# Second attention layer: first matrix blocks loaded in half-steps 48 to 50; first chunk's last block transposed within the output product

## The chip, the cores and the metric

The kernel runs on one core of one Trainium2 chip. The metric is the device time of one execution in microseconds (us): the median of several runs. The engines are named as in the profile: PE (matrix products), with PEld for its weight loads, DVE (VectorE), ACT (ScalarE), POOL (GpSimd) and SP (SyncE, which here only issues DMAs). A line number such as L955 is that of the kernel before.

## The reference, cut to what matters

Four layers, each with a residual sum: local dilated attention (A), Fourier mixing (B), and both once more. Everything is float32; S = 2048 rows, D = 640 columns.

```python
def _A_ref(x, wqkv, wo):
    H = 32; Dh = 20; W, dil = 8, 2
    qkv = (x @ wqkv).reshape(B, S, 3, H, Dh).transpose(2, 0, 3, 1, 4)
    ...
    logits = jnp.einsum("bhsd,bhswd->bhsw", q, kg) * scale
    logits = jnp.where(mask, logits, -1e9)
    attn = _softmax(logits, axis=-1)
    o = jnp.einsum("bhsw,bhswd->bhsd", attn, vg)
    return o.transpose(0, 2, 1, 3).reshape(B, S, D) @ wo

def _B_ref(x, dft_seq_re, dft_seq_im, dft_hid_re, dft_hid_im):
    a = jnp.einsum("bsd,ed->bse", x, dft_hid_re)
    b = jnp.einsum("bsd,ed->bse", x, dft_hid_im)
    return jnp.einsum("ts,bse->bte", dft_seq_re, a) - jnp.einsum("ts,bse->bte", dft_seq_im, b)

x = A_x
x = x + _A_ref(_layernorm(x), A_wqkv, A_wo)
x = x + _B_ref(_layernorm(x), ...)
x = x + _A_ref(_layernorm(x), A_wqkv, A_wo)
x = x + _B_ref(_layernorm(x), ...)
```

kg and vg hold, for each row, the keys and values of the eight rows 0, 2, ... 14 places before it.

## The kernel before

**Tiles and precision.** The rows lie in 4 chunks (c) of 4 blocks (j) of 128 rows. Float32 products are made of three passes over a high and a low half: a tile is split into a rounded high part (a cast on ACT) and the rest (a subtraction on DVE or POOL), and PE sums high by high, high by low and low by high.

**An attention layer** (`layer_a`; layers 0 and 2) runs in half-steps from -7 to 66. Half-step 2u + jp handles head group and chunk u, pair jp. Work is put into a plan, a dictionary by half-step and phase, with `at(step, phase, ...)`; the phases of a half-step are then played in a fixed order (PHASES), so each engine's queue has an order written out by hand. In a half-step stand: QKV products (`qkv_mm`, L362) with their evacuation by ACT (`qkv_evac`, L369) and stores; window loads of keys and values (`w_load`, L417, tile `win`, 5 buffers); the DVE products of `qk_mul` (L431) and `av_mul` (L469) with POOL's additions (L433, L484 to L486); the softmax; the output product with `wo` (`wo_mm`, L509) and the residual sum (`wo_add`, L159, stored by L523); layer norms of finished blocks (L884 and L888 make the high and low part of `xn`).

**The first z product.** The tail of an attention layer already does the first of the products of the Fourier layer behind it: z = xn transposed by one column block of the Fourier matrix, over 16 blocks of rows, z(0) to z(15), 15 matmuls each (`z_mm`, L955). `ZTHIRDS` says in which half-steps the thirds of each z(s) stand; for the second attention layer z(0) stands in half-step 50, z(1) and two thirds of z(2) in 51. A matrix block comes as a raw load (`c_load`, L911), a cast (`c_hi`, L915) and a subtraction (`c_lo`, L942) in the first attention layer, and ready-made as 512 KB from the DRAM buffer `c0b` (`c_get`, L933) in the second, one half-step before its first use. Its tile goes by `c_tag` into one of s0, s2 and s3 in turn, each a single buffer. The same buffers hold transposed blocks before: s2 and s3 blocks 2 and 3 of the last chunk's input, s0 the attention output of chunk 1's last block, which `wo_mm` reads in half-steps 48 and 49. A load into a buffer waits for the last reader of what was there, and SP issues its DMAs in order.

**Between the layers.** `early` (in `layer_a`) prepares chunk 0 of the second attention layer inside the last part of the Fourier layer (`LayerB.pair`): through hooks it loads, normalises and transposes blocks 0 to 3 (`xt`: PE transposes at L225 into the bank `pq`, a high part by ACT at L232, a low part by DVE at L236; each block in two parts, 2 and 3 transposes). The hooks ("y", k) stand behind the k-th fifth of the last y product, 12 matmuls each (`ymm`, L1033), and "end" behind everything. In `pair` only PE's order is given by hand; there, and where the two layers meet, a scheduler merges the two lists and orders the other engines. After a y product `yout` adds its banks to the residual (L1046, DVE) and takes its statistics (L151 and L153, ACT). `zt_put` (L1010 to L1015) splits a finished z into its two parts. In the last layer `x_whole` (L1078) adds the two parts of a stretch of `xn` again, into s1 or s2.

Of the kernel before, what the change touches and what calls it, by code (L numbers as in the profile page):

```python
# [28 lines left out]
NJ = 4  # L29
# [45 lines left out]
def tile_layers(ctx: ExitStack, tc: tile.TileContext, x, wqkv, wo, cs, wre, wim, out):  # L75
# [136 lines left out]
    def a_weights_q(q):  # L212
        wt = T([P, 2, KD, 3 * F], f"r1_{q}", F32R)
        for k in range(KD):
            split(wt[:, 0, k], wt[:, 1, k], wq_load1(q, k))
        return wt
# [25 lines left out]
    def layer_a(li, stats, handoff, prev):  # L242
# [21 lines left out]
        def at(step, phase, fn, *args):  # L264
            plan.setdefault((step, phase), []).append((fn, args))
# [5 lines left out]
        def x_load(c, j, tag="xa"):  # L271
            xnT[(c, j)] = load_x(xin[c], j, tag)
# [9 lines left out]
        def x_norm(c, j, fast=False):  # L282
            stats[c].apply(j, xnT[(c, j)], fast)

        def xt_pe(c, j, part, bank):
            if part == 0:
                xnT[(c, j, 1)] = T([P, 2, KD, P], f"s{j}", F32R)
            xnT[(c, j, "p", part)] = t_pe(xnT[(c, j)], part, bank)

        def xt_hi(c, j, part):  # L290
            t_hi(xnT[(c, j, 1)], part, xnT[(c, j, "p", part)])

        def xt_lo(c, j, part):
            t_lo(xnT[(c, j, 1)], part, xnT[(c, j, "p", part)])
# [278 lines left out]
        def early():  # L573
            def x_get(j):
                x_load(0, j)
                x_norm(0, j)

            def w0():
                with tc.issue_after(prev.dma.ins):
                    wq[0] = a_weights_q(0)  # L580

            def xt(j, part):
                xt_pe(0, j, part, "pq")
                xt_hi(0, j, part)
                xt_lo(0, j, part)

            prev.pair(
                NPAIR - 1,
                stats,
                {  # L590
                    2: lambda: (x_get(0), x_get(1)),
                    4: lambda: xt(0, 0),
                    5: lambda: (xt(0, 1), x_get(2)),
                    6: lambda: xt(1, 0),
                    7: lambda: (w0(), xt(1, 1), x_get(3)),
                    ("y", 1): lambda: xt(2, 0),
                    ("y", 2): lambda: xt(2, 1),
                    "end": lambda: (xt(3, 0), xt(3, 1)),
                },
            )  # L600
            for q in range(1, NQ):
                wq[q] = a_weights_q(q)
# [63 lines left out]
        if not first:  # L666
            early()
# [48 lines left out]
        for u in range(NG):  # L716
# [9 lines left out]
            for jp in range(2):  # L726
                s = 2 * u + jp
# [21 lines left out]
        for c in range(2):  # L749
# [10 lines left out]
            for j in range(NJ):  # L760
                t = LNS[ly][c] + (2 - c) * j
# [46 lines left out]
        for z in range(len(thirds) // 3):  # L808
            t = thirds[3 * z]
            if first and z in PRE:  # L810
                at(max(thirds[3 * z - 7] + 1, t - 3), "dmac", handoff.c_get, z)
            elif first:
                at(t - 2, "dmac", handoff.c_load, z)
                at(t - 1, "hi", handoff.c_hi, z)
                at(t - 1, "misc", handoff.c_lo, z, z < NJ)
            else:
                at(t - 1, "dmac", handoff.c_get, z)
            for p in range(3):
                at(thirds[3 * z + p], "pe3", handoff.z_mm, z, p)
        if first:  # L820
# [44 lines left out]
    class LayerB:  # L865
# [35 lines left out]
            nc.vector.tensor_scalar(self.xl[(c, j)], xr[(c, j)], nmean, rstd, op0=ALU.add, op1=ALU.mult)  # L901

        def c_tag(self, s, t=0):
            tags = ("s3", "s0", "s2") if self.li == 1 else ("s0", "s2", "s3")
            if t:
                return (tags[0], tags[-1 if self.li == 3 else 1])[s % 2]
            return tags[s % 3] if s < NST - 1 else "s1"

        def c_load(self, s, t=0):
# [382 lines left out]
    st0 = [None] * NC  # L1292
    b1, b2 = LayerB(1), LayerB(3)
    layer_a(0, st0, b1, None)
    st2 = [None] * NC
    b1.run(st2)
    layer_a(2, st2, b2, b1)
    b2.run(None)
    b2.ytile(NT - 1, 0, None)
# [56 lines left out]
```

## Time and profile before

| | us |
|---|---|
| three runs | 1796.40, 1798.74, 1799.93 |
| median | 1798.74 |
| the profiled execution, its own time | 1789.91 |
| its span, first to last instruction | 1788.0 |
| mean granted PE clock in it | 0.994 |

The profile is of one execution. In a row of a timeline stand the start, the duration, the engine, the line, the operation, out<-in by the program's names, shapes and a count; in brackets the idle time of the engine just before, and what ended it. Rows of the windows view give a stretch, its length, then busy time (and instructions) of PE, PEld, DVE, ACT and POOL, the granted PE clock, the share of time that the DMA engines were busy, and GB/s. By the windows view the first attention layer lies at about 0 to 395 us, the Fourier layer behind it at 395 to 925, the second attention layer at 880 to 1280, the last layer from there on.

### The profile page before, as it was taken

To read this page: it belongs to the slowest core of one execution; us is meant where nothing else is said; L and a number is where in the kernel's file an instruction comes from. 1 tells how busy PE (TensorE), PEld (TensorE's weight loads), DVE (VectorE), ACT (ScalarE), POOL (GpSimd) and SP (SyncE) were. 2 spreads that over 40 slices of the span, in tenths; PEclk is the share of its full clock that TensorE was granted. 3 is DMA by queue.
4 is the path that set the end of the run, shared out by engine and by line. 5 is a ranking of instruction groups with operands and counts; after the bars stand their busy time and mean duration, and the time that the engine had idled before them with its cause. 6 is when DMAs were issued, how large, how long until landed. Compare 5 with 4: busy or idle time off the path is not lost.

```text
span 1788.0 us, 26460 instructions
## 1 busy us (share of the span) xinstructions
PE 1741.6 (97%) x8798; PEld 1507.1 (84%) x8798; DVE 1381.9 (77%) x2139; ACT 813.1 (45%) x1690; POOL 634.8 (36%) x593
## 2 busy tenths in 40 slices
PE   9999998989999999999999999999999999999999
PEld 7889887778888888888888889878787888888888
DVE  6999998887767767767738999989777677677673
ACT  4664544454445445445623344444534443443441
POOL 4899999940000000000017998889300000000000
PEclk9999999999999999999999999999999999999999
DMA  7896678758778687777737866687687766876761
GB/s 248 286 313 211 203 210 269 252 183 282 268 255 264 239 274 252 240 267 249 225 125 224 265 213 218 208 293 248 228 295 259 261 223 224 267 230 228 253 208 52
DMA packets 271849, 425.15 MB, mean 238 GB/s; under 512 B 22592, under 2 KB 150592, under 8 KB 271456
## 3 DMA queue, kind: packets, MB, share of 16 engines
q1 hardware_dynamic: 268512, 421.49, 71.6%
q10 hardware_dynamic: 3200, 1.97, 0.4%
q8 instruction: 70, 1.15, 0.3%
q14 instruction: 67, 0.55, 0.1%
HBM read 338.23 MB, written 85.14 MB: 237 GB/s over the span
## 4 chain that ended last, share of the span: by engine, by line
PE 62%; DVE 14%; POOL 12%; DMA 7%; issue 3%; ACT 2%; SPq 0%; DVEq 0%; ACTq 0%; POOLq 0%
PE aux L1033 13%; PE m L362 12%; PE m L1122 9%; PE t L1122 9%; PE pq L1122 5%; PE xt L1122 5%; POOL pr L484 4%; DVE pr L431 3%; POOL pr L433 3%; DMA win<-cs_in 2%; DVE pr L469 2%; POOL pr L485 2%; PE m L955 2%; PE aux L509 2%; PE t L955 2%
## 5 line engine op out<-in xcount | busy, mean ns | idle before, releaser
L362 PE MATMUL m<-r,s 128*128 128x480 f32 x1920 | 436.5, 382 | 2.1 <-ACT s L232 1.6
L362 PEld LDWEIGHTS m<-r,s 128*128 128x128 f32 x1920 | 355.2, 188 | 55.8 <-ACT s L232 2.6
L1115 ACT CAST r<-win 128x512 fp32r<-128x512 f32 x248 | 151.1, 620 | 172.6 <-DVE win L1151 81.1
L174 POOL TENSOR_TENSOR stats<-stats,mhalf 128x1 f32<-128x1 f32 (+1 forms) x40 | 29.8, 746 | 558.4 <-ACT stats L170 549.1
L1033 PE MATMUL aux<-r2a,zo 128*128 128x320 f32 x768 | 226.4, 309 | 0.0
L484 POOL TENSOR_TENSOR pr<-pr 128x640 f32<-128x640 f32 x126 | 205.9, 1634 | 33.8 <-DVE pr L469 33.2
L1033 PE MATMUL aux<-pr,zo 128*128 128x320 f32 x704 | 208.2, 308 | 0.0
L431 DVE TENSOR_TENSOR pr<-pq,win 128x1280 f32<-128x1280 f32 x128 | 189.8, 1483 | 16.4 <-ACT pq L404 12.3
L1116 DVE TENSOR_TENSOR r<-win,r 128x512 fp32r<-128x512 f32 x248 | 167.4, 688 | 45.0 <-ACT r L1115 43.5
L469 DVE TENSOR_TENSOR pr<-pq,win 128x1280 f32<-128x1280 f32 x128 | 190.9, 1491 | 4.3
L433 POOL TENSOR_TENSOR pr<-pr 128x640 f32<-128x640 f32 x128 | 183.3, 1432 | 16.5 <-DVE pr L431 16.3
L1122 PE MATMUL m<-r,r 128*128 128x512 f32 x606 | 156.4, 392 | 0.8 <-DVE r L1116 0.8
L1033 PEld LDWEIGHTS aux<-r2a,zo 128*128 128x128 f32 x768 | 144.1, 188 | 2.0
L1122 PEld LDWEIGHTS m<-r,r 128*128 128x128 f32 x606 | 113.5, 188 | 26.6 <-DVE r L1116 1.5
L1033 PEld LDWEIGHTS aux<-pr,zo 128*128 128x128 f32 x704 | 132.2, 188 | 2.1
L955 PE MATMUL m<-s,r 128*128 128x512 f32 x384 | 120.1, 400 | 13.4 <-POOL s L942 4.9
L1122 PE MATMUL t<-r,r 128*128 128x512 f32 x483 | 130.7, 393 | 2.0 <-issue 1.2
L955 PE MATMUL t<-s,r 128*128 128x512 f32 x384 | 119.1, 398 | 2.3 <-DVE ot L1015 1.5
L439 DVE TENSOR_REDUCE lg<-pr 128x64 f32<-128x640 f32 x128 | 103.9, 812 | 18.2 <-POOL pr L433 17.8
L485 POOL TENSOR_TENSOR pr<-pr 128x320 f32<-128x320 f32 x126 | 113.0, 897 | 9.9
L1151 DVE TENSOR_TENSOR win<-win,win 128x512 f32<-128x512 f32 x110 | 75.7, 690 | 45.7 <-DMA win<-cs_in 43.9
L1122 PEld LDWEIGHTS t<-r,r 128*128 128x128 f32 x483 | 90.5, 188 | 23.4 <-issue 1.6
(285 smaller groups left out, 3227.8 us busy)
## 6 DMA issues: line engine op xcount, KB each, us to landing
win<-cs_in SPq DMA_DIRECT2D x354, 256.0 KB, 4.2
r<-xc SPq DMA_DIRECT2D x240, 256.0 KB, 4.4
win<-kvb SPq DMA_DIRECT2D x96, 440.0 KB, 4.3
xa<-cs_in SPq DMA_DIRECT2D x122, 256.0 KB, 4.2
win<-kvb SPq DMA_DIRECT2D x64, 360.0 KB, 5.3
xc<-stg SPq DMA_DIRECT2D x40, 512.0 KB, 3.4
kvb<-stg SPq DMA_DIRECT2D x60, 320.0 KB, 4.7
xr<-xs SPq DMA_DIRECT2D x41, 320.0 KB, 3.6
```

The source lines that it names most:

```text
L362: nc.tensor.matmul(mt[g][:, : 3 * F], st[:, a, k], wq[q][:, b, k], start=n == 0, stop=n == 14)
L431: nc.vector.tensor_tensor(pr, q, wview(u, jp, 0, [[1, FE]]), op=ALU.mult)
L433: nc.gpsimd.tensor_tensor(pv[:, :, 0:10], pv[:, :, 0:10], pv[:, :, 10:20], op=ALU.add)
L439: nc.vector.tensor_reduce(lgs[u][:, 2 * jp : 2 * jp + 2].rearrange("p j w h -> p (j w h)"), prq.pop((u, jp))[:, :, 0:10], axis=AX.X, op=AL ...
L469: nc.vector.tensor_tensor(pr.rearrange("p j w (h d) -> p j w h d", d=DH), lgs[u][:, 2 * jp : 2 * jp + 2].unsqueeze(4).to_broadcast([P, 2, ...
L484: g.tensor_tensor(pr[:, :, 0:4], pr[:, :, 0:4], pr[:, :, 4:8], op=ALU.add)
L485: g.tensor_tensor(pr[:, :, 0:2], pr[:, :, 0:2], pr[:, :, 2:4], op=ALU.add)
L955: self.last = nc.tensor.matmul(self.z[t][k], self.xn[c][:, a, j, k * P : (k + 1) * P], self.ct[s][:, b], start=s == 0 and i == 0, stop=s = ...
L1033: self.last = nc.tensor.matmul(self.ym[e][:, :320], zt[(k, a, ri)][:, j2 * P : (j2 + 1) * P], w[:, e * 320 : (e + 1) * 320], start=(k, a, ...
L1115: nc.scalar.copy(hi, raw)
L1116: nc.vector.tensor_tensor(lo, raw, hi.bitcast(F32), op=ALU.subtract)
L1122: nc.tensor.matmul(bank, w(a, kb), hl[b], start=start and (a, b) == (0, 0), stop=stop and (a, b) == (1, 0),)
```

## The change

Four edits. The last two groups of transposes of `early` go from the hook "end" to the hooks ("y", 3) and ("y", 4). In the first attention layer the subtraction for z(11) and z(12) goes to POOL instead of DVE (`early=True` of `c_lo`). In the second, `c_get` for z(0), z(1) and z(2) is put into half-steps 48, 49 and 50 (before: 49, 50 and 50). And the tags of the last Fourier layer's first product begin with s2 instead of s0, while those of its second product stay as they were (s0, s3).

```diff
@@ early() @@
                     ("y", 1): lambda: xt(2, 0),
                     ("y", 2): lambda: xt(2, 1),
-                    "end": lambda: (xt(3, 0), xt(3, 1)),
+                    ("y", 3): lambda: xt(3, 0),
+                    ("y", 4): lambda: xt(3, 1),
@@ layer_a: the plan of the z products @@
             elif first:
                 at(t - 2, "dmac", handoff.c_load, z)
                 at(t - 1, "hi", handoff.c_hi, z)
-                at(t - 1, "misc", handoff.c_lo, z, z < NJ)
+                at(t - 1, "misc", handoff.c_lo, z, z < NJ or z in (11, 12))
             else:
-                at(t - 1, "dmac", handoff.c_get, z)
+                at(min(t - 1, 48 + z) if z < 3 else t - 1, "dmac", handoff.c_get, z)
@@ LayerB @@
         def c_tag(self, s, t=0):
-            tags = ("s3", "s0", "s2") if self.li == 1 else ("s0", "s2", "s3")
             if t:
-                return (tags[0], tags[-1 if self.li == 3 else 1])[s % 2]
+                return (("s3", "s0") if self.li == 1 else ("s0", "s3"))[s % 2]
+            tags = ("s3", "s0", "s2") if self.li == 1 else ("s2", "s0", "s3")
             return tags[s % 3] if s < NST - 1 else "s1"
```

## The prediction

> **What bounds the kernel now.** The page first: it says which engine has no room.
>
> ```profile
> span 1788.0 us, 26460 instructions
> PE 1741.6 (97%) x8798; PEld 1507.1 (84%) x8798; DVE 1381.9 (77%) x2139; ACT 813.1 (45%) x1690; POOL 634.8 (36%) x593
> ```
>
> PE is idle for 1788.0 − 1741.6 = 46.4 us in all, so an edit can win only by removing some of that idle time, or by removing stretches in which PE is busy but slow. I went from the waits of line 955 (z_mm) to the timelines around the four places where the two built programs differ. The windows view, one row for each stretch (last three columns: granted PE clock, DMA share, GB/s), shows the dearest place, the start of the second layer's z product:
>
> ```profile
> 1172.00:1174.00 2.00, 1.43 (x12) 1.19 (x10) 1.93 (x3) 1.49 (x5) 1.84 (x4) 1.00 0.00 0
> 1176.50:1183.00 6.50, 6.43 (x15) 4.74 (x15) 5.53 (x8) 1.78 (x6) 6.26 (x7) 0.54 1.00 335
> ```
>
> The DMA engines carry nothing from 1172 to 1174 and are then full; PE does 15 matmuls in 6.5 us at clock 0.54. PE's and SP's timelines say why:
>
> ```profile
> 1170.71 2.36 PE L509 MATMUL aux<-r2a,s 128*128 128x320 f32 x15
> 1173.96 0.44 PE L335 MATMUL t<-r,nident 128*128 128x384 f32 x1 [0.57 <-ACT r L331]
> 1176.47 2.92 PE L955 MATMUL m<-s,r 128*128 128x512 f32 x6 [2.07 <-DMA s<-c0b]
> 1184.12 0.73 PE L955 MATMUL m<-s,r 128*128 128x512 f32 x2 [1.19 <-DMA s<-c0b]
> 1190.07 1.04 PE L327 MATMUL aux<-ident,zo 128*128 128x128 f32 x8
> ...
> 1166.47 0.92 SPq L417 DMA_DIRECT2D win<-kvb  x2
> 1173.10 0.32 SPq L933 DMA_DIRECT2D s<-c0b  x1
> 1176.34 0.93 SPq L523 DMA_DIRECT2D xs<-xa  x1
> 1177.32 1.97 SPq L933 DMA_DIRECT2D s<-c0b  x2
> ```
>
> Block 0 is issued at 1173.10, when line 509 has finished with its old tenant of s0 (1170.71 + 2.36); PE waits 2.07 for it. Blocks 1 and 2 are issued behind the store of 1176.34; PE waits 1.19 for block 1. The lost time here is 2.07 + 1.19 + about 3.0 of half speed (15 matmuls from 1176.47 to 1182.93, 6.46; 25 take 1190.07 − 1184.12 = 5.95, so 15 at full clock 3.5) = 6.2 us.
>
> **Part 1, the blocks.** The rotation of tags for the second layer becomes s2, s0, s3. Block 0 goes to s2, free since the matmuls of the block before last, so its issue moves from 1173.10 to just ahead of the two window loads of 1166.47; it lands before the DMA engines fall idle. Block 1 now wants s0 and takes the place at 1173.10; block 2 stays behind the store of 1176.34, which waits for a VectorE add that nothing moves. From issue to use block 0 took 1176.47 − 1173.10 = 3.4 on idle DMA engines; block 1, by the chain of waits, 6.75 on full ones:
>
> ```profile
> 1177.32 6.75 DMA s<-c0b
> ```
>
> So z(0) runs from 1174.4 to 1177.9 without a wait, z(1), landed at 1176.5, to 1181.4, and z(2) waits for block 2: the bytes in front of it are those that stood in front of block 1, so it lands at 1177.32 + 6.75 = 1184.1. z(2) began at 1184.12 + 3.5 = 1187.6 before; PE is now 3.5 us ahead, but with a new gap of 1184.1 − 1181.4 = 2.7 us. What such a gap does to the clock:
>
> ```profile
> 356.56 6.12 PE L509 MATMUL aux<-r2a,s 128*128 128x320 f32 x30 [2.10 <-DVE xa L159]
> 307.03 4.56 PE L509 MATMUL aux<-r2a,s 128*128 128x320 f32 x30
> 282.92 1.43 PE L955 MATMUL m<-s,r 128*128 128x512 f32 x5 [1.91 <-POOL s L942]
> ```
>
> After 2.10 idle the same 30 matmuls took 1.56 more; after 1.91 the next five ran at full rate. Both gaps over 2 us brought half clock, so I charge 1.3 (1.56 less what falls into the gap itself): PE is 2.2 ahead at 1190.07. The Trainium skill ("TensorE: Matmul & The Clock Gate", Part 1: The HAM clock gate) has the clock halve only after at least one idle window of about 3.4 us; by that the charge would be 0 and the sum 0.8 better. The half rate agrees with 0.54 above; the 2.10 us gap does not agree with the length.
>
> Does the lead last? VectorE and GpSimd set the pace from 1190 on:
>
> ```profile
> 1189.14 1.49 DVE L431 TENSOR_TENSOR pr<-pq,win 128x1280 f32<-128x1280 f32 x1 [3.53 <-DMA win<-kvb]
> 1192.14 0.38 DVE L460 TENSOR_REDUCE pq<-lg 128x16 f32<-128x128 f32 x1 [1.51 <-ACT lg L447]
> 1195.35 1.58 POOL L484 TENSOR_TENSOR pr<-pr 128x640 f32<-128x640 f32 x1 [3.23 <-DVE pr L469]
> ```
>
> The 3.53 wait shrinks by what one block (512 KB at the 335 GB/s above, 1.5) no longer puts in front of the window load; L460 waits for ACT, whose exp stands behind copies of PE's transposes of 1190.07. So this chain comes 1.5 + 1.51 = 3.0 earlier at most, and 2.2 if PE is. I take **−2.2**; bounds 0 (nothing passes the attention chain) and −6.2 (block 2 in time, the clock stays up).
>
> **Part 2, the transposes.** The last block's two groups of PE transposes (2 and 3, line 225) move from after the y product into it. In the built order one more thing moves with them: ten of the second QKV group's matmuls (line 362) now stand before the last twelve of line 1033, where seven stood behind them.
>
> ```profile
> 891.35 0.39 PE L1033 MATMUL aux<-r2a,zo 128*128 128x320 f32 x1
> 894.94 1.69 PE L362 MATMUL m<-r,s 128*128 128x480 f32 x7
> 899.20 0.70 PE L362 MATMUL m<-r,s 128*128 128x480 f32 x2 [1.04 <-ACT s L232]
> 900.80 3.10 PE L362 MATMUL m<-r,s 128*128 128x480 f32 x13 [0.57 <-ACT s L232]
> ...
> 893.52 0.46 ACT L232 CAST s<-pq 128x384 fp32r<-128x384 f32 x1
> 896.19 0.89 DVE L1046 TENSOR_TENSOR xr<-aux,xr 128x320 f32<-128x320 f32 x2
> 897.11 0.74 ACT L151 ACTIVATE junk<-xr 128x640 bf16<-128x640 f32 x1 [1.28 <-DVE xr L1046]
> 898.80 0.35 ACT L232 CAST s<-pq 128x256 fp32r<-128x256 f32 x1
> 899.16 0.55 ACT L369 COPY stg<-m 128x480 f32<-128x480 f32 x1
> ```
>
> Two waits, 1.04 + 0.57 = 1.61, should go. But those ten need the copy of 893.52, done at 893.98. Twelve of line 1033 end at 891.35 + 1.8 = 893.15 (24 fill 891.35 to 894.94), so PE waits 0.85 there. Then ten matmuls (2.4 by the row of 894.94), the transposes and twelve of line 1033 (1.8) end at 898.3. In ACT's queue the copy of the second transposes stands behind L151, L369 and L153, and L151 waits for the adds behind line 1033's end: some 0.6 later (the second of the two adds, 0.45, and the hand-overs), 898.9. From L151 to the copy it is 898.80 − 897.11 = 1.69, plus 0.5 for the L369 now between: the copy runs from 901.1 to 901.55 and the 13 matmuls start at 901.6 instead of 900.80: **+0.8**. Bounds: −1.6 (both waits go, none comes) and +2.4 (0.8 and one halving, 1.56).
>
> **Part 3, blocks 11 and 12 of the first layer.** Their subtraction (line 942) moves from VectorE to GpSimd.
>
> ```profile
> L942 POOL TENSOR_TENSOR s<-stg,s x4: 1266/1272/1288, 281.6 to 304.4; 128x512 fp32r<-128x512 f32 x4
> L942 DVE TENSOR_TENSOR s<-stg,s x4: 681/1362/1903, 349.6 to 370.1; 128x512 fp32r<-128x512 f32 x4
> ...
> 363.39 0.49 DVE L159 SCALAR_TENSOR_TENSOR xa<-aux,xa 128x320 f32<-128x320 f32 x1 [0.84 <-DMA xa<-x_in]
> 368.76 0.62 ACT L915 CAST s<-stg 128x512 fp32r<-128x512 f32 x1 [4.48 <-DMA stg<-cs_in]
> 370.22 1.94 POOL L484 TENSOR_TENSOR pr<-pr 128x640 f32<-128x640 f32 x1 [1.81 <-DVE pr L469]
> 374.48 0.73 PE L955 MATMUL m<-s,r 128*128 128x512 f32 x2 [0.54 <-DVE r L888]
> 382.11 0.73 PE L327 MATMUL pq<-ident,zo 128*128 128x128 f32 x4 [0.89 <-POOL zo L486]
> ```
>
> VectorE is freed of about 1.36 twice, GpSimd gets 1.27 twice. The first is lost, since VectorE then waits for the load of 363.39 anyway. The second lets VectorE's next products, and the GpSimd work that waited 1.81 for them, start some 1.2 earlier; GpSimd's own 1.27 fits under those waits. PE's 0.54 goes, and the wait at 382.11 ends 0.9 earlier, since ACT, held by the load at 368.76, gives back a part. I take **−0.9**; bounds 0 and −1.4.
>
> **Part 4, an unnamed move.** With s2 free one block earlier, the first whole-tile sum of the last layer (line 1078) stands in VectorE's queue before the last head's tree (484 to 486), not after it.
>
> ```profile
> 1266.33 0.54 DVE L486 TENSOR_TENSOR zo<-pr 128x160 f32<-128x160 f32 x1
> 1267.15 0.60 PE L327 MATMUL pq<-ident,zo 128*128 128x128 f32 x4
> 1278.25 1.23 DVE L1078 TENSOR_TENSOR s<-r 128x1024 f32<-128x1024 f32 x1
> ```
>
> The tree ends at 1266.87, PE takes it at 1267.15; with 1.23 in front it ends at 1268.10: **+0.95** on PE. Where the sum stood, nothing waited for it. Bounds 0 and +1.3.
>
> **Sum:** −2.2 + 0.8 − 0.9 + 0.95 = −1.35 us. The profiled execution lasted 1789.91 (span 1788.0 and 1.9 around it), 8.8 below the median of the three runs, 1798.74; I carry the difference over unscaled: **1797.4 us**. From 0.2% (3.6 us; runs of before spread over 3.5) the difference can be told from none.
>
> **Rivals.** (a) *The clock stays up* in the new gap of part 1, as after the 1.91 gap: the lead is 3.0 and the sum −2.15: 1796.6. (b) *Block 2 lands in time*: its place in the queue improves by a block, the whole 6.2 is recovered: −6.2 + 0.85 = −5.35: 1793.4. For it: DMA is empty until 1174. Against: the issue behind the store at 1176.34 does not move. (c) *The transposes do what the change says*: −1.6 in place of +0.8, sum −3.75: 1795.0. For it: ACT's copy of the first transposes now comes before L151. Against: the copy of the second stands behind it. (d) *Slower*: the two new gaps of part 2 (0.85 and about 1.4, within 8.5 us) halve PE's clock there. Price 1.56 for one spell, 3.0 for one like 1176.5 to 1183; from 1.35 on the kernel is slower: up to 1800.4. Against: the present gaps there, 1.04 and 0.57, do nothing.
>
> **How the numbers follow.** Forecast 0.36, (a) 0.16, (b) 0.18, (c) 0.16, (d) 0.14. Faster by over 0.2% (below 1795.1) is nearly all of (b), half of (c) and, with the scatter of runs, a fifth of the forecast and (a): 0.35. Slower by over 0.2% (above 1802.3) needs (d) with scatter, or a bound of part 2 and part 4 together: 0.10. Within: 0.55. The range runs from (b) less its scatter, 1792.4, to (d), 1800.6.
>
> **What would show it.** In the changed profile: line 933's first row near 1166.5, no wait at z(0), clock 1.00 from 1174 to 1181, then a DMA wait of 2 to 3 before z(2); a line 362 wait of 0.85 near 893 and a larger one before the 13; PE's wait for VectorE near 374 gone; line 1078 before 484 and a wait of PE for line 486 near 1265. No wait before z(2), or none before the 13, would make it wrong.

## The result, and the profile after

| | before | changed |
|---|---|---|
| first series, median (20 runs each) | 1796.30 | 1791.13 |
| second series, median (28 and 10 runs) | 1793.12 | 1790.10 |
| the profiled execution, its own time | 1789.91 | 1791.85 |
| its span | 1788.0 | 1790.0 |

The ratio of changed to before is 0.9977, with a 95% interval of 0.9967 to 0.9986, in the first series and 0.9982 (0.9972 to 0.9993) in the second: 4.1 us and 3.2 us faster. The prediction said 1797.4 us and 1.35 us faster, so the sign was right, the gain too small, and 1791.13 lies 1.3 below the low end of the range, 1792.4. The two profiled executions stand the other way round: the one of before took 1789.91, 6.4 below the median of the twenty timed runs of before. The traces are therefore read stage by stage, and most of the work below is about what one execution can show. Line numbers above 598 are one higher in the changed kernel (942 becomes 943, 955 becomes 956, 1033 becomes 1034).

The page of the changed kernel, its span and busy times:

```profile
span 1790.0 us, 26461 instructions
PE 1740.7 (97%) x8798; PEld 1506.0 (84%) x8798; DVE 1380.2 (77%) x2137; ACT 813.0 (45%) x1690; POOL 636.4 (36%) x595
```

PE's idle time is 49.3 us, where it was 46.4. Nothing on the page tells the two kernels apart; the four stages do.

**Part 1.** Timelines of PE and of SP at the start of the second layer's z product:

```profile
1174.08 2.36 PE L509 MATMUL aux<-r2a,s 128*128 128x320 f32 x15
1177.61 1.56 PE L956 MATMUL m<-s,r 128*128 128x512 f32 x6
1181.11 0.63 PE L956 MATMUL m<-s,r 128*128 128x512 f32 x2
1187.64 0.73 PE L956 MATMUL m<-s,r 128*128 128x512 f32 x2 [2.86 <-DMA s<-c0b]
1191.00 1.70 PE L327 MATMUL aux<-ident,zo 128*128 128x128 f32 x8
...
1169.58 0.38 SPq L934 DMA_DIRECT2D s<-c0b  x1
1176.47 0.32 SPq L934 DMA_DIRECT2D s<-c0b  x1
1179.73 0.87 SPq L523 DMA_DIRECT2D xs<-xa  x1
1180.65 1.24 SPq L934 DMA_DIRECT2D s<-c0b  x1
```

Block 0 is asked for 4.5 us before the group of line 509 that held it back, so z(0) (1177.61) and z(1) start without a wait. Block 1 has taken the place behind that group (1176.47), block 2 stands behind the store, and PE waits 2.86 for it. From line 509 to line 327 it is 1191.00 − 1174.08 = 16.92, against 19.36 before: 2.44 less. Most of the lead lasts: from the same group to the 18 matmuls of line 509 near 1265 us it takes 1265.46 − 1174.08 = 91.38, against 1264.41 − 1170.71 = 93.70 before, 2.32 less.

**Part 2.** Timeline of PE where ten matmuls of line 362 now stand ahead of line 1034's last ones, and of ACT, which makes their operands; the last two rows are ACT's in the kernel before:

```profile
895.16 4.00 PE L362 MATMUL m<-r,s 128*128 128x480 f32 x10 [2.08 <-ACT s L232]
900.98 1.26 PE L362 MATMUL m<-r,s 128*128 128x480 f32 x5
904.22 3.10 PE L362 MATMUL m<-r,s 128*128 128x480 f32 x13 [1.65 <-ACT s L232]
...
892.85 0.60 ACT L126 ACTIVATE r<-win 128x480 fp32r<-128x480 f32 x1 [0.76 <-DMA win<-wqkv_in]
894.14 0.60 ACT L126 ACTIVATE r<-win 128x480 fp32r<-128x480 f32 x1 [0.24 <-DMA win<-wqkv_in]
894.65 0.46 ACT L232 CAST s<-pq 128x384 fp32r<-128x384 f32 x1
903.70 0.46 ACT L232 CAST s<-pq 128x384 fp32r<-128x384 f32 x1
```

```profile
891.87 0.60 ACT L126 ACTIVATE r<-win 128x480 fp32r<-128x480 f32 x1 [0.64 <-DMA win<-wqkv_in]
893.01 0.60 ACT L126 ACTIVATE r<-win 128x480 fp32r<-128x480 f32 x1
```

The first copy of line 232 ran from 893.52 before. Now it comes at 894.65. Two roundings of weights (line 126) stand ahead of it in both kernels; in this execution they start at 892.85 and 894.14 instead of 891.87 and 893.01, both of them when a load of weights lands. The two waits of 1.04 and 0.57 have become 2.08 and 1.65, and the ten matmuls took 4.00 where the row of seven at full clock (1.69) gives 2.4.

**Parts 3 and 4.** Timeline of PE at lines 889 and 486 in the first layer, then at line 486 in the second, and VectorE's rows for the latter:

```profile
372.46 0.73 PE L956 MATMUL m<-s,r 128*128 128x512 f32 x2 [0.25 <-DVE r L889]
380.10 0.73 PE L327 MATMUL pq<-ident,zo 128*128 128x128 f32 x4 [0.89 <-POOL zo L486]
1269.27 0.55 PE L327 MATMUL pq<-ident,zo 128*128 128x128 f32 x3 [0.38 <-DVE zo L486]
...
1265.05 1.65 DVE L1079 TENSOR_TENSOR s<-r 128x1024 f32<-128x1024 f32 x1
1266.62 1.49 DVE L484 TENSOR_TENSOR pr<-pr 128x640 f32<-128x640 f32 x1
1268.89 0.33 DVE L486 TENSOR_TENSOR zo<-pr 128x160 f32<-128x160 f32 x1
```

PE's wait for line 889 has shrunk from 0.54 to 0.25 and the wait for line 486 at 380.10 is still 0.89, but it ends 2.0 earlier. Of these 2.0, 1.45 are half clock that before had behind line 509's wait at 356 us and this execution has not (6.12 against 4.67 for the same 30 matmuls). In the second layer line 1079 stands ahead of the tree, whose end PE awaits; from the first group of line 509 (18 matmuls) to the second it took 3.80 before and 4.82 now, 1.02 more.

### The profile page after: what moved, and what is told of

It reads as the page before. It is cut to its first block, busy times and chain, and to the rows that moved or that the text cites. A ratio compares the mean times of both kernels' runs of the same rounds, so it can differ in the third digit from the quotient of the medians.

```text
span 1790.0 us, 26461 instructions
## 1 busy us (share of the span) xinstructions
PE 1740.7 (97%) x8798; PEld 1506.0 (84%) x8798; DVE 1380.2 (77%) x2137; ACT 813.0 (45%) x1690; POOL 636.4 (36%) x595
## 4 chain that ended last, share of the span: by engine, by line
PE 59%; DVE 15%; POOL 10%; DMA 9%; issue 3%; ACT 2%; SPq 0%; ACTq 0%; DVEq 0%; POOLq 0%
PE aux L1034 13%; PE m L362 11%; PE m L1123 10%; PE t L1123 10%; PE pq L1123 5%; PE xt L1123 5%; DVE pr L431 4%; POOL pr L484 3%; DVE pr L469 3%; POOL pr L433 2%; DMA win<-cs_in 2%; POOL pr L485 2%; PE aux L509 2%; DMA xc<-stg 1%; DVE lg L439 1%
## 5 line engine op out<-in xcount | busy, mean ns | idle before, releaser
L433 POOL TENSOR_TENSOR pr<-pr 128x640 f32<-128x640 f32 x128 | 183.8, 1436 | 14.1 <-DVE pr L431 13.7
L369 ACT COPY stg<-m 128x480 f32<-128x480 f32 x128 | 70.9, 554 | 81.6 <-PE m L362 58.9
```

The source lines that it names most:

```text
L433: nc.gpsimd.tensor_tensor(pv[:, :, 0:10], pv[:, :, 0:10], pv[:, :, 10:20], op=ALU.add)
```

## The experiments

Sixteen runs follow: eight new kernels, two of them twice, and three more runs each of before and of the changed kernel. "Stage" means the time between the same two instructions of PE in two traces, and its change is counted from the first profiled execution of before.

### The parts alone

Blocks and tags (parts 1 and 4), twice:

```diff
-                at(t - 1, "dmac", handoff.c_get, z)
+                at(min(t - 1, 48 + z) if z < 3 else t - 1, "dmac", handoff.c_get, z)
...
-            tags = ("s3", "s0", "s2") if self.li == 1 else ("s0", "s2", "s3")
+            tags = ("s3", "s0", "s2") if self.li == 1 else ("s2", "s0", "s3")
```

> The kernel before with the new rotation of tags and the earlier issues of blocks 0 to 2 only (parts 1 and 4 of the prediction); lines 598 and 815 stay as they were. Theory A (the gain is this part, and larger in a typical execution than the -2.2 + 0.95 of the prediction): -3 us or more beside the kernel before, most of the -4 to -5 of the whole change. Rival B (this part is worth what the prediction said, and the gain is elsewhere): -1.3 us. In the trace by both: no wait before z(0) and z(1) of line 955, a DMA wait of 2.5 to 3 before z(2), half clock behind it, and line 1078 ahead of the tree of lines 484 to 486 with PE about 1 us later.

> Parts 1 and 4 alone once more (first series: -1.1 us, between -3.4 and +1.3). Theory A (the stage of the z product gains 2.9 us, as the mean of four traces with and four without it says, and part 4 costs 0.9): -2.0 us. Rival J (this part carries the whole gain of the changed kernel): -3.5 us or more.

Measured: ratio 0.9994 (0.9981 to 1.0007) and 0.9992 (0.9980 to 1.0004), that is 1.1 and 1.4 us faster. This is rival B in the first and between A and none in the second. J's 3.5 lies at the edge of the second interval (3.6) and beyond that of the first (3.4), so it is unlikely. In the first trace line 1078's delay cost 2.77 in its stage, with a stretch at half clock in it, in the second 0.82.

The transposes (part 2):

```diff
-                    "end": lambda: (xt(3, 0), xt(3, 1)),
+                    ("y", 3): lambda: xt(3, 0),
+                    ("y", 4): lambda: xt(3, 1),
```

> The kernel before with the two early transposes of the last block only (part 2). Theory A (this part costs time): +0.8 us if PE's clock stays up behind the two new waits, +2.4 to +3.7 with one stretch at half clock, as in the profiled execution of the changed kernel, where first line 1033 to the last 13 matmuls of line 362 took 13.1 us against 9.45. Rival C (in a typical execution the two waits of 1.04 and 0.57 go and the part gains): -1.6 us, and that stretch under 9.5 us.

Measured: 1.0004 (0.9990 to 1.0018), 0.7 us slower, theory A's first figure. Its stage took 1.45 more than in the first execution of before, without half clock. C falls for this execution; how typical that first execution is comes below.

The two subtractions (part 3), twice:

```diff
-                at(t - 1, "misc", handoff.c_lo, z, z < NJ)
+                at(t - 1, "misc", handoff.c_lo, z, z < NJ or z in (11, 12))
```

> The kernel before with the subtraction of blocks 11 and 12 of the first layer on GpSimd only (part 3). Theory A: -0.5 us (what the two traces show once their clocks are made equal), within 0.9 of none. Rival D (half clock behind the 2.1 us wait of line 509 near 356 us comes from what this edit leaves on VectorE, and goes with it): -2 us, by 1.5 of clock and 0.5 of waits.

> Part 3 alone once more (first series: -0.7 us, between -3.0 and +1.4). Theory A (it gains 0.9 to 1.2 where both clocks are equal): -1.0 us. Rival J (it gains nothing that reaches the end, since 350 to 480 us gives back in some traces what 350 to 385 gained): 0.

Measured: 0.9996 (0.9983 to 1.0008) and 0.9989 (0.9980 to 0.9998), 0.7 and 2.0 us faster. Half clock at 356 us is there in both traces, so rival D falls. A stands; none at all, which is rival J of the second run, lies just outside that run's interval (0.4 to 3.6 faster).

The tags without the earlier half-steps (the edit beside the version with blocks and tags):

```diff
-                at(min(t - 1, 48 + z) if z < 3 else t - 1, "dmac", handoff.c_get, z)
+                at(t - 1, "dmac", handoff.c_get, z)
```

> The kernel before with the new rotation of tags only: the blocks are asked for at their old half-steps, block 0 at 49, but into s2, which is free by then, so that it no longer waits for line 509 of the group before. Theory A (what held block 0 was its buffer, not its half-step): its issue still comes before 1170 us and its wait of 2.07 us is gone; block 1 then wants s0 at its old half-step behind the store of xs, so that the wait for it stays; -1 us or so with part 4's +1 in it. Rival B (the half-step held it too): block 0 issued near 1173 and no gain, +1 us from part 4 alone.

Measured: 1.0002 (0.9986 to 1.0017). Block 0 was asked for at 1168.15 and z(0) did not wait, so what held it was its buffer, not its half-step. Blocks 1 and 2 were both issued at 1176.89, behind the store, and PE waited 3.88 before z(1):

```profile
1182.42 1.22 PE L955 MATMUL m<-s,r 128*128 128x512 f32 x2 [3.88 <-DMA s<-c0b]
```

The wait has moved from block 0 to block 1. The stage takes 19.82, about what it took in the first execution of before (19.36). The earlier half-step of block 1 is as much part of the gain as the tags.

### Without the transposes

```diff
-                    ("y", 3): lambda: xt(3, 0),
-                    ("y", 4): lambda: xt(3, 1),
+                    "end": lambda: (xt(3, 0), xt(3, 1)),
```

> The changed kernel with line 598 put back: the last block's transposes at the end again. Theory A (the transposes cost 1.4 to 1.7 us in their stage): 1 to 2 us faster than the changed kernel, and first line 1033 to the 13 matmuls of line 362 back under 10 us, or 11.7 with a stretch at half clock there. Rival C: 1.6 us slower than the changed kernel.

Measured: 0.9976 (0.9966 to 0.9985), 4.3 us faster than before, beside 3.2 for the whole change in the same series. The direction is A's and not C's, but the 1.1 between them is within the intervals. In this trace the old order, too, had a long wait and then half clock:

```profile
901.39 0.70 PE L362 MATMUL m<-r,s 128*128 128x480 f32 x2 [1.77 <-ACT s L232]
902.98 4.64 PE L362 MATMUL m<-r,s 128*128 128x480 f32 x13 [0.57 <-ACT s L232]
```

The 13 matmuls took 4.64, where they took 3.10 in the first execution; the 1.77 stood at 1.04 there.

### The same two kernels again

> The kernel before once more, unchanged, timed as a variant: what it shows is how much two series of the same kernel differ. Expected: ratio 1.000 within 0.0013. Its trace is a second execution of before. Theory A (before's first profiled execution was a lucky one in its waits): more waits or half-clock stretches than the first (6 stretches of 3.41 us at half clock), span 1790 to 1793 us. Rival (that execution was typical): span within 1 us of 1788.0 and no part of it more than 1.7 us away.

> The changed kernel once more. Sum of its parts by the four single-part series so far (blocks -0.8, transposes +0.4, subtractions -1.6, by medians): -1.1 us, with about 2 us of uncertainty. Theory A (the parts add, and the -4 us of the first series is mostly scatter between series): 1 to 2 us below before. Rival E (the parts help each other): -4 us again, and a trace in which one stage is over 2 us shorter than in both single-part traces.

> A further execution of the kernel before, for its stages. Theory A (the first profiled execution had the stage of the second layer's z product unusually short, and part 1 gains about 3 us in a typical one): from line 509's group ahead of z(0) to line 327 behind z(2) it takes 20 to 22 us, as in the other four traces without part 1 (19.9 to 22.8), not 19.4. Rival K (that execution was typical there): 19.0 to 19.7.

> A further execution of before, as the one of e13_before_look: 20 to 22 us in that stage by theory A, 19.0 to 19.7 by rival K. With theory G (a stretch of the fixed grid with more than half of it idle on PE is followed by half clock) two or three stretches at half clock there.

> A further execution of the changed kernel, for its stages. Theory A: 17 to 18 us in the stage of the z product (16.1 to 18.8 in the five traces with part 1), one stretch at half clock behind z(2)'s wait in most; 890 to 905 us 1.4 us longer than in an execution of before without half clock there, and 3 to 3.7 longer with one. Rival K: 16.9 as in the first.

> A further execution of the changed kernel, as the one of e15_after_look: by theory A 17 to 18 us in the stage of the z product with one stretch at half clock, and 1.4 us (no half clock) or 3 to 3.7 us (with it) more than before from 890 to 905 us. Rival K: 16.9 in the stage of the z product.

Before against itself gave 1.0006 (0.9995 to 1.0017), an interval that holds 1, as it should. Its trace is that of the longest of its twelve runs (span 1799.3, nine windows at half clock), so that the first execution was not typical, as theory A said, but this one is not either. The changed kernel gave 3.2 us, between A's 1 to 2 and E's 4; no stage of its trace was over 2 us shorter than in both single-part traces, so E has no mechanism.

The stage of the z product, from line 509 to line 327, in the seven traces with part 1 and the seven without it (single-part kernels included):

| | us | mean |
|---|---|---|
| without part 1 | 19.36, 19.73, 19.87, 20.90, 21.39, 21.80, 22.76 | 20.8 |
| with part 1 | 16.11, 16.92, 17.27, 17.50, 17.71, 17.90, 18.30 | 17.4 |

The first execution of before is the shortest of its seven. Theory A said 20 to 22 for the two further looks: one gave 21.80, the other 19.73, which is K's figure. Two or three stretches at half clock were expected there in the second; it had one. The two further looks at the changed kernel gave 17.50 and 17.71, as A said. What differs between the executions of before is read from PE's timeline. The execution with 21.80:

```profile
1173.60 2.36 PE L509 MATMUL aux<-r2a,s 128*128 128x320 f32 x15
1179.32 1.66 PE L955 MATMUL m<-s,r 128*128 128x512 f32 x6 [2.03 <-DMA s<-c0b]
1187.33 1.22 PE L955 MATMUL m<-s,r 128*128 128x512 f32 x2 [4.25 <-DMA s<-c0b]
1195.40 1.04 PE L327 MATMUL aux<-ident,zo 128*128 128x128 f32 x8
```

Both blocks land at nearly the same distance as in the first execution: z(1) starts 1187.33 − 1173.60 = 13.7 after the group of line 509, against 1184.12 − 1170.71 = 13.4. But in the first execution the half clock fell on z(0) (its first six matmuls took 2.92, here 1.66), where PE would only have waited longer for block 1: 1.19 there, 2.66 to 4.25 in the six others. The half clock cost next to nothing. Here it reaches past the start of z(1), where nothing hides it: two matmuls take 1.22 instead of 0.73. Four of the six others have it there and take 20.9 to 22.8, the two that don't take 19.7 and 19.9.

All four stages, as mean change from the first execution of before, by the 18 traces there are (in stage 1 without the four kernels that alter it in other ways):

| stage | without the part | with it | difference |
|---|---|---|---|
| 1, z product | +1.5 (7 traces) | −2.0 (7) | −3.4 |
| 2, transposes, lines 1033 and 362 | +1.4 (12) | +1.7 (6) | +0.3 |
| 3, subtractions, 330 to 385 us | −1.2 (8) | −1.6 (10) | −0.5 |
| 4, line 1078 ahead of the tree | 0.0 (9) | +1.1 (9) | +1.1 |

The sum is −2.5. In stage 2, too, the first execution was the shortest of the twelve; five of the twelve had half clock there, and one of the six with the change. In stage 3 it was the longest of its eight. There one execution with the part had three stretches at half clock; without it the mean with the part is −2.1 and the difference −0.9. Theory A's 3 to 3.7 with half clock in stage 2 was seen once, in the first trace of the changed kernel (3.67); the others gave 0.7 to 1.6.

### What sets the clock

Apart from the one that the end of each trace cuts, all half-clock stretches in these traces are 3.41 us long or twice or three times that, and within one execution they start at multiples of 3.413 us from each other. So I laid that grid over every trace. Windows of the changed kernel (after the stretch and its length: busy time and count of PE, PEld, DVE, ACT and POOL; granted clock, DMA share, GB/s), three around line 362's wait and two around the wait of line 509 at 356 us, then the latter two in before:

```profile
891.98:895.39 3.41, 1.33 (x9) 1.07 (x8) 2.15 (x5) 2.26 (x6) 0.00 (x0) 1.00 0.68 200
895.39:898.80 3.41, 3.41 (x10) 2.77 (x10) 2.02 (x5) 0.98 (x2) 0.00 (x0) 0.50 0.39 121
898.80:902.22 3.42, 3.42 (x23) 3.14 (x22) 1.96 (x5) 1.42 (x3) 0.00 (x0) 1.00 0.00 0
...
352.73:356.14 3.41, 1.71 (x8) 1.05 (x6) 3.24 (x7) 0.00 (x0) 2.90 (x4) 1.00 0.36 108
356.14:359.55 3.41, 3.02 (x20) 3.03 (x21) 3.34 (x8) 0.43 (x1) 3.25 (x4) 1.00 0.56 167
```

```profile
352.98:356.40 3.42, 1.48 (x7) 0.87 (x5) 3.35 (x6) 0.22 (x1) 2.98 (x4) 1.00 0.37 108
356.40:359.81 3.41, 3.25 (x12) 3.25 (x13) 3.41 (x7) 0.21 (x1) 3.06 (x3) 0.50 0.66 196
```

A window with PE busy 1.33 or 1.48 of 3.41 is followed by one at 0.50; one with 1.71 is not. The wait itself was the same in both kernels, 2.09 and 2.10: it lay 0.2 us differently on the grid. Over the 18 traces, of the full-clock windows with at least 1.8 us idle on PE 78 of 80 were followed by half clock, of those with 1.65 to 1.8 idle 4 of 20, and of those with less 3 of 9176. That is a pattern; the experiment that makes it a cause fills the wait before z(2) with work that nothing uses:

```diff
+        def filler(n, bank):
+            pb = pt([P, 512], bank)
+            for _ in range(n):
+                nc.tensor.matmul(pb[:, :320], nident, wo_s["w"][:, 0, 0, :320], start=True, stop=True)
...
+            if z == 2 and not first:
+                at(t, "pe3", filler, 10, "aux0")
```

> The changed kernel with ten filler matmuls (128x320, into a free bank that nothing reads) on PE between z(1) and z(2) of the second layer, where PE waits 2.86 us (3.09 in the second trace) for block 2. They add work that the result does not use and leave the wait's end where it is. Theory G (PE's clock is set on a fixed grid of 3.413 us: a stretch of the grid in which PE is idle more than about half, 1.7 us, makes the next stretch run at half clock): the fillers take about 1.45, the idle time before z(2) falls to about 1.4, no stretch at half clock follows, and from z(1)'s start to line 327 it takes 1.4 to 1.7 us less than in the changed kernel's two traces (both had one there). Rival H (half clock comes with the wait for the DMA itself, such as power or memory traffic, not with PE's idle time): the stretch at half clock stays. Against before by the series: 1 to 1.5 us more than the changed kernel's gain.

Measured: 0.9971 (0.9959 to 0.9983), 5.2 us faster than before. PE's timeline of this kernel (line 520 is the filler, 963 the z product):

```profile
1181.16 1.63 PE L520 MATMUL aux<-r2a,nident 128*128 128x320 f32 x10
1184.30 0.73 PE L963 MATMUL m<-s,r 128*128 128x512 f32 x2 [1.51 <-DMA s<-c0b]
1186.74 1.04 PE L327 MATMUL aux<-ident,zo 128*128 128x128 f32 x8
1188.08 0.38 PE L335 MATMUL aux<-ot,nident 128*128 128x256 f32 x1 [0.30 <-ACT s L331]
```

Filler and rest of the wait together are as long as the wait was (1.63 + 1.51 = 3.1, against 2.86 to 3.09). Behind it there is no half clock: from z(2)'s first matmul to line 335 it takes 1188.08 − 1184.30 = 3.78, in the changed kernel's first two traces 5.16 and 5.29. In the seven traces with part 1 and no filler it is 5.16 to 6.23 in the six with half clock and 3.77 in the one without. One trace could therefore be luck; the twelve timed runs are not (mean granted clock 0.9964, against 0.9952, table below). Theory G holds and H falls: extra work made the kernel faster, with the DMA engines as full as before, and the half clock at 356 us follows a wait for VectorE, not for a DMA. The grid windows of the wait and behind it, first in the changed kernel, then in this one:

```profile
1185.49:1188.90 3.41, 1.26 (x5) 1.05 (x6) 3.21 (x4) 0.00 (x0) 3.17 (x6) 1.00 1.03 403
1188.90:1192.31 3.41, 3.41 (x13) 2.83 (x12) 1.21 (x1) 0.21 (x1) 3.33 (x3) 0.51 1.05 386
```

```profile
1182.08:1185.49 3.41, 1.90 (x10) 1.46 (x10) 3.34 (x5) 0.16 (x1) 3.17 (x5) 1.00 1.03 404
1185.49:1188.91 3.42, 3.07 (x19) 2.30 (x17) 1.30 (x2) 1.53 (x7) 3.34 (x4) 1.00 1.05 388
```

PE is busy 1.90 instead of 1.26 in the first window, and the second runs at 1.00 instead of 0.51.

The timed runs carry the same account, since each lists its mean granted clock. (1 − clock) × span is the most that half clock can have cost; it is less where a wait follows, as in the first execution of before.

| kernel | runs | mean clock | lost at most, us | mean time less that |
|---|---|---|---|---|
| before | 105 | 0.99397 | 10.8 | 1782.6 |
| changed | 32 | 0.99516 | 8.7 | 1782.3 |
| blocks and tags alone | 24 | 0.99467 | 9.6 | 1782.6 |
| subtractions alone | 24 | 0.99388 | 11.0 | 1781.3 |
| transposes alone | 12 | 0.99400 | 10.8 | 1782.6 |
| changed, with filler | 12 | 0.99642 | 6.4 | 1782.0 |

The 105 runs of before are those of all series but the first, for which no clock is listed. Against them the changed kernel is 2.5 us faster in the mean, and at most 2.1 of them are clock; but 20 of its 32 runs are of the first series. In the second series alone it is 3.5 in the mean, with 2.0 of clock.

### A version that is faster than both

The waits that the change leaves can go: z(1)'s block into s3, free after line 362, z(2)'s into s0, both ahead of the store; the transposes back at the end; line 1078 held behind the tree.

```diff
-                at(min(t - 1, 48 + z) if z < 3 else t - 1, "dmac", handoff.c_get, z)
+                at(min(t - 1, (48, 49, 49)[z]) if z < 3 else t - 1, "dmac", handoff.c_get, z)
...
-            tags = ("s3", "s0", "s2") if self.li == 1 else ("s2", "s0", "s3")
+            tags = ("s3", "s0", "s2") if self.li == 1 else ("s2", "s3", "s0")
...
+            with tc.issue_after(self.tree.ins):
+                nc.vector.tensor_tensor(self.whole[side], v[:, 0], v[:, 1], op=ALU.add)
```

> Without the transposes, and with blocks 1 and 2 put right as well: the second layer's rotation is s2, s3, s0, so that block 1 goes to s3 (free after line 362 of block 3, 1174.1 in the changed kernel's trace) and block 2 to s0 (free at 1176.4), both asked for in half-step 49, ahead of the store of xs; the second product's tags are s3, s0; and line 1078's first sum is held behind the tree of lines 484 to 486. Theory A (the wait of 2.86 before z(2), the half clock behind it and the early line 1078 are separate losses): no wait before z(0), z(1), z(2), no half clock from 1174 to 1192, -4.5 there, nothing lost at 1268; against the changed kernel -2.9 - 1.3 - 1.0 - 1.5 = -6 us at most, -3 if the attention chain behind 1190 sets the pace. Rival F (the window loads now stand behind one more block): VectorE's line 431 near 1189 waits 1.5 us longer and gives all of it back.

Measured (7 runs): 0.9965 (0.9951 to 0.9979), 6.3 us faster than before and 3.1 faster than the changed kernel in the same series. PE's and VectorE's timelines:

```profile
1172.89 2.36 PE L509 MATMUL aux<-r2a,s 128*128 128x320 f32 x15
1176.42 1.56 PE L955 MATMUL m<-s,r 128*128 128x512 f32 x6
1185.76 1.04 PE L327 MATMUL aux<-ident,zo 128*128 128x128 f32 x8
...
1189.46 1.49 DVE L431 TENSOR_TENSOR pr<-pq,win 128x1280 f32<-128x1280 f32 x1 [1.54 <-DMA win<-kvb]
1264.45 1.21 DVE L1078 TENSOR_TENSOR s<-r 128x1024 f32<-128x1024 f32 x1
```

The stage takes 12.87 instead of 16.92, without a wait or half clock, and stage 4 loses nothing. VectorE's wait for its window load is 1.54, against 3.53 before, so F falls. By 1262 us 2.7 of the lead over before's first execution was lost again, on the attention chain; theory A's "3 if that chain sets the pace" is what came. The gain lies in waits rather than in the clock, whose mean over the seven runs is 0.9947, lower than that of the changed kernel: other waits, which this version keeps, still halve it.

Last, fillers at three waits of the first layer, none of which the change touched:

```diff
+                if first and (c, j) == (1, 3):
+                    at(a, "pe", filler, 8, "aux0")
...
+            if z == 2 and first:
+                at(t, "pe3", filler, 6, "aux0")
...
+                if self.li == 1 and t == 0 and s == 0 and p == 0 and n == 1:
+                    for _ in range(4):
+                        nc.tensor.matmul(self.z[t][4], self.xn[c][:, 0, j, :P], self.ct[s][:, 0], start=True, stop=True)
```

> The version of e8_best with fillers at three waits of the first layer that are followed by half clock in most traces: eight 128x320 ahead of line 335's two matmuls near 262 us (wait 2.37), four 128x512 behind z(0)'s first matmul near 281 (1.91), six 128x320 ahead of z(2) near 293 (1.96). Theory G (half clock follows a grid stretch with more than 1.7 us idle): the half-clock stretches near 264 and 283 to 295 go, only the one or two near 300 and 356 stay; 2 fewer stretches, 1.7 us each: about -3 us beside e8_best. Rival H: the same stretches at half clock, and a time equal to e8_best or longer by a part of the fillers' 3 us. Rival I (the first layer there waits for VectorE and GpSimd, so a faster PE only waits longer): the half clock goes but the time stays.

Measured (5 runs): 0.9955 (0.9943 to 0.9967), 8.1 us faster than before, with a mean granted clock of 0.9966. The half clock near 264 and from 283 to 295 is gone from the trace and that at 302, 356.6 and 902.8 us is left; each of the 17 other traces has half clock near 264, from 283 to 296, or at both. Beside the 6.3 this is 1.8 more, less than the 3 expected and not certain across two series. A part went to rival I: line 509 at 301 us, which ACT feeds, waited longer, where it waited 1.66 in before:

```profile
300.86 5.32 PE L509 MATMUL aux<-r2a,ot 128*128 128x320 f32 x24 [2.98 <-ACT s L350]
```

## Why the prediction missed, step by step

**The step that failed** is the base of the sum: "The profiled execution lasted 1789.91 ..., 8.8 below the median of the three runs, 1798.74; I carry the difference over unscaled." It treated one execution's stages as the kernel's, and the level of three runs as its level. Both were off. The level: twenty runs put before at 1796.3, which is 2.4 of the 6.3 by which 1797.4 missed (and in the later series before stood at 1792.9 to 1793.7, so the level itself moves). The other 3.9 are the difference, 5.2 by these medians (4.1 by the ratio) instead of 1.35. Of them the traces account for about 1.2: stage 1 of the first execution was the shortest of seven, so that the term of part 1, −2.2, should have been −3.4; stage 2 was the shortest of twelve, and +0.8 should have been +0.3; part 3 gave 0 to 0.4 less than its −0.9, and part 4 0.1 more than its +0.95. The remaining 2.7 (1.6 by the ratio) no trace explains.

**Part 1 (−2.2 predicted).** The order was right in every row: block 0 ahead of the window loads, no wait at z(0) and z(1), a wait before z(2) of 2.86 (2.7 predicted), half clock behind it in six of seven traces. In the first pair it gave −2.44. Its size is −3.4 ± 1.1 (twice the standard error) over seven traces each. Mis-sized was the loss before, "2.07 + 1.19 + about 3.0 of half speed". Its 6.2 is right for that execution: without waits and half clock the stage takes 12.87, and 19.36 − 12.87 = 6.5. But there the half speed lay where PE waited for block 1 anyway; in four of the seven executions it reaches past the start of z(1) and the stage takes 1.5 to 3.4 longer, so that the mean loss is 20.8 − 12.9 = 7.9. The question whether the lead lasts was answered rightly: VectorE's wait for its window load shrank from 3.53 to 2.33, and 2.3 of the 2.44 were left near 1265 us.

**Part 2 (+0.8).** The first step failed in a detail: "those ten need the copy of 893.52, done at 893.98". It took the copy's time from one execution, but ahead of the copy stand two roundings that wait for their loads. Counted from the first of the last 24 matmuls of line 1033, the copy starts after 2.17 in that execution, and after 2.13 to 4.16 in the 18 traces. So the wait was 2.08 in the first trace and 0.64 to 1.55 in the five others with the change, not 0.85 each time. The second wait, 1.65, was near the 1.4 predicted. But the old order is no better on average: its own waits (1.04 and 0.57 in the quoted rows, 1.77 and 0.57 in another trace) bring half clock in five executions of twelve. The part costs +0.3 by the traces, +0.7 (−1.8 to +3.2) by its own series: none that can be told.

**Part 3 (−0.9)** is right within its uncertainty: −0.5 to −0.9 by traces, −0.7 and −2.0 by series. "PE's 0.54 goes" holds in the main: that wait is 0.54 to 1.30 in the eight traces without the part and at most 0.53 in nine of the ten with it. **Part 4 (+0.95)** is right: +1.02 in the first pair, +1.1 in the mean; holding line 1078 back removes it.

**Rivals.** (a), the clock stays up in the new gap: one trace of seven. (b), block 2 in time: no trace; the waits before z(2) are 2.78 to 3.18. (c), the transposes gain 1.6: in none of six traces, where their stage takes 0.7 to 3.7 more than in the first execution of before. (d), the new gaps of part 2 halve the clock: in the first trace as described (4.00 for the ten matmuls), but in one of six. Its price was right for an execution, wrong for the kernel, since what decides is where the grid happens to lie, and the old order runs the same risk.

**The clock.** "Both gaps over 2 us brought half clock, so I charge 1.3" took for certain what depends on the grid: behind the new wait it came in six traces of seven. The rule of the Trainium skill weighed there ("TensorE: Matmul & The Clock Gate", Part 1: The HAM clock gate) gives a free-running window of 3413 ns, and that agrees with the 3.413 us of these traces. I had used it as a gap length. Read as one whole window without work it would not agree either: with 1.8 us idle in a window, little more than half, 78 of 80 were followed by half clock.

**What stays open.** The stages add up to −2.5 (−2.9 without the trace with three stretches at half clock in stage 3), the series say −3.2 and −4.1 with intervals of about 1.8 either way. For parts 1 and 4 the stages say −2.3, their two series −1.1 and −1.4. No further stage was found; chance is enough for the rest, but that was not shown.

## What to carry to other kernels

A sum against one profiled execution needs that execution's place among others, stage by stage: take several traces, and where the first one is the shortest, as here in two stages, expect more from removing its waits (and less where it is the longest, as in a third). A wait on PE costs its own length and, if it can empty more than half of a 3.4 us window, up to 1.7 us more behind it (half of 3.41; 1.45 in the rows at 356 us), more likely the longer it is; so a wait may be worth filling with useless matmuls, if no other engine sets the pace behind it, and half clock that lies ahead of a later wait is free. A tag is part of the schedule: giving a block another buffer moved its load past two others, and a VectorE sum in the next layer with it.

## What the hardware showed that was not expected

- PE's clock is decided on a grid of 3.413 us whose place differs from execution to execution: about 1.8 us idle inside one window halves the clock of the next (78 of 80 times). Two waits of 2.09 and 2.10 us at the same instruction differed by this alone (4.67 us for 30 matmuls behind the one, 6.12 behind the other).
- Adding ten matmuls to a stage made it about 1.4 us shorter than with half clock. By its granted clock before loses up to 10.8 us of 1793 to such windows, six of them in a run.
- From one execution to the next the same stage of the same kernel takes 19.4 to 21.8 us (four traces of before) though its blocks land at nearly the same distances: what moves is on which side of a wait the half clock falls.
